# Transposing q and k of chunks 4 to 7 by DMA in a fused attention and ELU kernel, with eight shared PSUM banks and a new order of work

## The chip, the core and the metric

The kernel runs on one core of a Trainium2 chip. A core has five engines that run side by side: TensorE (PE, with its weight loads shown as PEld), VectorE (DVE), ScalarE (ACT), GpSimd (POOL) and SyncE (SP). Sixteen DMA engines move data between HBM and the on-chip memory SBUF. Matrix products land in PSUM, which has eight banks. The metric is device microseconds of one execution, as the median of several.

## The reference

The reference is a linear attention with decay, followed by a two-layer network with an ELU. All inputs are float32: q, k, v of shape (4, 8, 768, 64) for 4 batches, 8 heads, 768 positions and head size 64; a decay lam for each head; weights of 512x2048 and 2048x512.

```python
for b in range(nb):                       # blocks of 64 positions
    intra = einsum('bhic,bhjc->bhij', qb, kb) * Dmask
    intra = einsum('bhij,bhjd->bhid', intra, vb)
    inter = einsum('bhid,bhde->bhie', qb * lam_pow, kv_state)
    out[:, :, sl] = intra + inter
    kv_state = lam_block * kv_state + einsum('bhsd,bhse->bhde', kb * rev_pow, vb)
x = out.transpose(0, 2, 1, 3).reshape(3072, 512)
h = x @ w_in
g = where(h > 0, h, exp(min(h, 0)) - 1)
return g @ w_out
```

## The kernel before

The kernel cuts the 768 positions into 6 blocks of 128, so that there are 24 chunks of 128 tokens: chunk g belongs to batch g mod 4 and block g div 4. The state of a batch goes from chunk g to chunk g + 4. Chunks 0 to 3 are worked alone, and from chunk 4 on two chunks are loaded, and go through the network's first layer, as a pair (`GROUPS`, `LOADS`). Everything is float16 between float32 accumulations.

The order of all work is written out by hand in one string, `PROGRAM`, and the loop at L453 emits one word after another; no scheduler changes it. Each engine runs its own words strictly in that order and waits, by semaphore, for what a word needs. The words, with the chunk or tile in their number:

- `Lq`, `Lk`, `Lv` (L240): POOL issues a load of q, k or v that casts float32 to float16; `wi`, `wo` (L245, L251) load one of eight tiles of each weight the same way. All of these share one DMA queue, q0 on the page. `Hq0` and `Cq0` load q of chunk 0 raw from SP and cast it on DVE.
- `T`, `Tq`, `Tk` (L264): PE transposes q and k, four 128x128 blocks for each, into PSUM; `tq` (L272) moves q to SBUF on DVE, scaled by the decay `qs`, and `tk` (L276) moves k on ACT. They need the identity `idn` (L193), which needs the two `iota` of POOL.
- `Dq`, `Dk` (L280): instead, SP issues a DMA transpose from SBUF to SBUF, once the load has landed. q then is not scaled by `qs`, and the scaling is done when the chunk's result is moved (L328, on DVE; where q was scaled already, L326 on ACT moves it). Chunks 8 to 23 go this way. These transposes and the stores share the queue q1.
- `S` (L287) the scores, `s` (L294) the mask on DVE, `P` (L304, L310) the products with v and with the state, `p` (L326 or L328) the result to SBUF as `xt`.
- `kd` (L332) and `M` (L342) decay k and the state on POOL; `U` (L354, L366) the state's update on PE, `u` (L379, L381) its addition on DVE; `z` clears a state.
- `A` (L392): a part of the first layer, one PSUM bank of 512 columns; `x` (L400) exp and `r` (L403) relu on ACT, `m` (L408) the ELU on DVE into `g`.
- `B` (L422): a quarter of the second layer of a chunk, in a bank that the chunk keeps for all four; `o` (L431) moves it to SBUF, `st` (L436) stores it from SP. `R` is the last 128 columns of the last chunk.

A word after `@` names the PSUM bank. Before, A takes one of two banks of its own by turns ("H"), and the other words name one of M0, M1, A, B, C and D. The tiles `qn2`, `kn2`, `vn2` of pairs have four buffers each, `qT` and `kT` five: a word that takes a buffer waits for the last reader of the tile that had it.

Of the kernel before, what the change touches and what calls it, by code (L numbers as in the profile page):

```python
# [7 lines left out]
FP32 = mybir.dt.float32  # L8
FP16 = mybir.dt.float16
# [8 lines left out]

BUFS = {'qn1': 4, 'kn1': 4, 'vn1': 4, 'qn2': 4, 'kn2': 4, 'vn2': 4, 'qT': 5, 'kT': 5, 'pp': 6, 'kd': 8, 'stt': 8, 'xt1': 4, 'xt2': 2, 'xt4': 2, 'e': 3, 'g': 40, 'osb512': 4}

ON = {'z0.0', 'z2.0', 'z1.0', 'o23', 'z3.0'}

# [4 lines left out]


PROGRAM = (
# [53 lines left out]
)  # L85


# [1 line left out]
def kernel(  # L89
# [11 lines left out]
    nc = tc.nc  # L101
# [8 lines left out]
    FB = 4  # L110
# [48 lines left out]
        return sb.tile(shape, dtype, tag=tag, name=name, bufs=BUFS.get(tag, 1))  # L159

    def bank(tag, shape, dtype, name):
        return ps.tile(shape, dtype, tag=f"ps{tag}", name=name, bufs=2 if tag == "H" else 1)

    def ln(_):
        nc.scalar.activation(loglam[:], lam_b[:], AF.Ln)
# [216 lines left out]
                out=new, in0=stt.pop((g, hh))[r], in1=psU.pop((g, hh)), op=ALU.add  # L382
            )

    def first_product(g0, j):
        n = size_of[g0]
        assert {f"p{g0 + i}" for i in range(n)} <= done
        pH = psH[g0, j] = bank("H", [128, FB * 128], FP32, f"psH{g0}_{j}")
        for f in range(FB // n):
            i, w = divmod(j * (FB // n) + f, 2)  # L390
            for kk in range(NHP):
                nc.tensor.matmul(  # L392
                    pH[:, f * n * 128 : (f + 1) * n * 128],
                    lhsT=wi16[i][:, kk, w * 128 : (w + 1) * 128],
                    rhs=xg[g0][:, kk, :], start=(kk == 0), stop=(kk == NHP - 1),
                )
# [38 lines left out]
        t0 = b * S + c * L  # L435
        nc.sync.dma_start(out=out[t0 : t0 + 128, cols], in_=osb.pop((g, cols.start))[:])  # L436

    rest = []

    def last_columns(banks):  # L440
        cols = slice(CUT, DM)
# [11 lines left out]
    for word in words:  # L453
# [15 lines left out]
        elif kind in ("tq", "tk"):  # L469
            evacuate_t(kind[1], *a)  # L470
        elif kind in ("Dq", "Dk"):
            transpose_dma(kind[1], *a)
        elif kind == "S":
            scores(*a, banks)
        elif kind == "P":
            products(*a, banks)
        elif kind == "U":
            update_products(a, banks)
        elif kind == "B":
            second_product(*a, banks)  # L480
        elif kind == "o":
            evacuate_o(*a, psM.pop(*a)[:, cols_of(*a)], cols_of(*a), name in ON)
        elif kind == "st":
            store(*a, cols_of(*a))
        elif kind == "R":
            last_columns(banks)
        elif kind == "oR":
            evacuate_o(LAST, rest[0][:], slice(CUT, DM), False)
        elif kind == "stR":
            store(LAST, slice(CUT, DM))  # L490
        else:
            {
                "wi": load_wi, "wo": load_wo, "z": zero_state, "s": masked, "p": evacuate_p,
                "kd": decay_k, "M": decay_state, "u": update, "A": first_product, "x": exp,
                "r": relu, "m": elu,
            }[kind](*a)

# [29 lines left out]
```

## Time and profile before

| what | value |
| --- | --- |
| median of 3 runs | 215.63 us (215.39 to 217.02) |
| the profiled execution's own time | 215.01 us |
| its span, first to last instruction | 213.2 us |
| matmuls | 2048, mean granted clock 1.0 |
| first matmul, end of the last | 6.13 us, 210.13 us |
| DMA moved | 24.59 MB, 101976 packets |

The profile is of one execution. Busy time of an engine is the time in which it had an instruction in work; PE's instructions overlap, so that a busy PE says when it had work and not how fast it went. The distance from start to start of two words on PE, where nothing was waited for, says what a word costs. The view of waits says, for each instruction that its engine stood idle for, what came last before it started. The DMA share counts the packets' own times over 16 engines; packets of two queues overlap, and it can be over 1. "Landing" of a DMA is the time at which its completion is seen.

### The profile page before, as it was taken

The page shows a single profiled execution, that of the slowest core. Times are in us where ns is not written, and L with a number is a line of the kernel's source. Part 1 is how long each engine was busy: PE and PEld are TensorE (multiplying, and loading weights), DVE is VectorE, ACT ScalarE, POOL GpSimd, SP SyncE. Part 2 cuts the span into 40 slices and gives each one's busy share as a digit, 9 for nine tenths or more (in the row PEclk, how much of TensorE's full clock was granted, in tenths as well). Part 3 has the DMA queues.
Part 4 walks back from the last instruction along what each step waited for, and adds up shares of the span by engine and source line. Part 5 has one row for each costly group of instructions (what it writes and reads, how often), then busy time and mean ns, then how long its engine had stood idle before and what let it go on. Part 6 is the DMA issues. An engine that isn't in the chain of part 4 may idle for free.

```text
span 213.2 us, 5052 instructions
## 1 busy us (share of the span) xinstructions
PE 199.2 (93%) x2048; PEld 138.5 (65%) x2048; DVE 129.6 (61%) x223; ACT 127.9 (60%) x245; POOL 96.6 (45%) x115
## 2 busy tenths in 40 slices
PE   0599989999999999999989999999999999999994
PEld 0378767677677766767657677667666776666662
DVE  3877764385877866788538676366558665353321
ACT  4436766568776765585554865665674565556731
POOL 7999965599994995376902691000000000000000
PEclk9999999999999999999999999999999999999999
DMA  5999999999999999969997999146110000021042
GB/s 95 152 181 184 197 194 182 158 145 151 161 120 166 127 169 150 148 101 113 187 148 80 158 187 127 25 130 145 25 52 0 0 16 36 3 103 46 0 152 98
DMA packets 101976, 24.59 MB, mean 115 GB/s; under 512 B 92608, under 2 KB 99008, under 8 KB 101952
## 3 DMA queue, kind: packets, MB, share of 16 engines
q0 software_dynamic: 79760, 13.50, 83.5%
q1 hardware_dynamic: 22192, 10.76, 23.9%
q8 instruction: 16, 0.26, 0.5%
q14 instruction: 8, 0.07, 0.1%
HBM read 27.27 MB, written 6.29 MB: 157 GB/s over the span
## 4 chain that ended last, share of the span: by engine, by line
PE 64%; POOL 17%; DMA 15%; issue 1%; ACT 0%; SPq 0%; POOLq 0%
PE psM L422 29%; PE psH L392 28%; DMA kn<-in_k_dram 5%; DMA vn<-in_v_dram 4%; DMA qT<-qn 4%; POOL wi L245 3%; POOL kn L240 3%; POOL wo L251 3%; POOL kd L332 3%; DMA out_dram<-osb 3%; POOL qn L240 3%; PE psO L304 2%; POOL vn L240 2%; PE psO L310 2%; PE psS L287 2%
## 5 line engine op out<-in xcount | busy, mean ns | idle before, releaser
L408 DVE SCALAR_TENSOR_TENSOR g<-e,psH 128x512 f16<-128x512 f32 x96 | 65.6, 685 | 61.3 <-ACT psH L403 61.0
L392 PE MATMUL psH<-xt,wi 128*128 128x256 f16 (+1 forms) x896 | 97.6, 259 | 0.9 <-DMA wi<-in_moe_w_in_dram 0.8
L400 ACT ACTIVATE e<-psH 128x512 f32<-128x512 f32 x96 | 57.2, 596 | 67.4 <-PE psH L392 67.0
L422 PE MATMUL psM<-wo,g 128*128 128x512 f16 (+1 forms) x384 | 92.7, 377 | 0.2 <-ACT osb L431 0.2
L392 PEld LDWEIGHTS <-wi 128*128 128x128 f16 x896 | 77.5, 99 | 22.8 <-DMA wi<-in_moe_w_in_dram 1.3
L403 ACT ACTIVATE psH<-psH 128x512 f32<-128x512 f32 x96 | 56.9, 594 | 0.0
L422 PEld LDWEIGHTS <-g 128*128 128x128 f16 x384 | 36.4, 98 | 31.4 <-issue 0.4
L294 DVE TENSOR_TENSOR pp<-psS,mask 128x512 f16<-128x512 f32 x48 | 31.4, 682 | 7.6 <-PE psS L287 7.5
L332 POOL TENSOR_TENSOR kd<-kn,ks 128x512 f16<-128x512 f16 x20 | 20.8, 1049 | 13.0 <-DMA kn<-in_k_dram 12.5
L342 POOL TENSOR_TENSOR stt<-st,upp 64x256 f32<-64x256 f16 x32 | 19.6, 612 | 7.4 <-DVE st L381 5.9
L240 POOL DMA_DIRECT2D vn<-in_v_dram x14 | 15.7, 1121 | 9.0 <-PE psO L310 9.0
L431 ACT COPY osb<-psM 128x512 f32<-128x512 f32 x23 | 13.4, 588 | 5.7 <-PE psM L422 4.8
L240 POOL DMA_DIRECT2D kn<-in_k_dram x14 | 15.5, 1107 | 1.6 <-DMA wi<-in_moe_w_in_dram 1.4
L240 POOL DMA_DIRECT2D qn<-in_q_dram x13 | 14.4, 1110 | 0.1
L381 DVE TENSOR_TENSOR st<-stt,psU 64x256 f16<-64x256 f32 x32 | 13.0, 415 | 0.8 <-PE psU L366 0.3
L304 PE MATMUL psO<-pp,vn 128*64 128x128 f16 x192 | 12.5, 229 | 0.3 <-DMA vn<-in_v_dram 0.3
L304 PEld LDWEIGHTS <-vn 128*64 128x64 f16 x192 | 10.0, 114 | 2.6 <-issue 1.6
L328 DVE TENSOR_TENSOR xt<-psO,qs 128x512 f16<-128x512 f32 x16 | 10.7, 683 | 1.1 <-PE psH L392 0.6
L287 PE MATMUL psS<-qT,kT 64*128 64x128 f16 x192 | 8.4, 228 | 2.8 <-DMA qT<-qn 1.1
L310 PE MATMUL psO<-qT,st 128*64 128x128 f16 x160 | 10.3, 219 | 0.0
L287 PEld LDWEIGHTS <-kT 64*128 64x128 f16 x192 | 5.9, 98 | 5.8 <-issue 3.6
L310 PEld LDWEIGHTS <-st 128*64 128x64 f16 x160 | 9.0, 110 | 0.0
(45 smaller groups left out, 65.1 us busy)
## 6 DMA issues: line engine op xcount, KB each, us to landing
out_dram<-osb SPq DMA_DIRECT2D x23, 256.0 KB, 2.9
qn<-in_q_dram POOLq DMA_DIRECT2D x10, 256.0 KB, 8.0
kn<-in_k_dram POOLq DMA_DIRECT2D x10, 256.0 KB, 6.5
vn<-in_v_dram POOLq DMA_DIRECT2D x10, 256.0 KB, 7.0
wi<-in_moe_w_in_dram POOLq DMA_DIRECT2D x8, 256.0 KB, 6.4
wo<-in_moe_w_out_dram POOLq DMA_DIRECT2D x8, 256.0 KB, 7.4
kn<-in_k_dram POOLq DMA_DIRECT2D x4, 128.0 KB, 4.7
vn<-in_v_dram POOLq DMA_DIRECT2D x4, 128.0 KB, 5.5
```

Source lines behind the costliest of these rows:

```text
L240: nc.gpsimd.dma_start(out=t[:].rearrange("p b h d -> p (b h) d"), in_=source(w, g0, load_n[g0]))
L287: nc.tensor.matmul(psS[g, hh][:, hp, :], lhsT=tr["k", g][r, hp, :], rhs=tr["q", g][r, hp, :], start=True, stop=True,)
L294: nc.vector.tensor_tensor(out=p[:], in0=psS.pop((g, hh))[:], in1=mask[:, hh::2, :], op=ALU.mult)
L304: nc.tensor.matmul(po[r, hp, :], lhsT=of("v", g)[:, 2 * hp + hh, :], rhs=pp[g, hh][:, hp, :], start=True, stop=(cb == 0), skip_group_check ...
L310: nc.tensor.matmul(po[r, hp, :], lhsT=st[b][cb % 2][:, hp, r], rhs=tr["q", g][:, hp, :], start=False, stop=True, skip_group_check=True,)
L332: nc.gpsimd.tensor_tensor(out=kds[g][:], in0=of("k", g), in1=ks[:].unsqueeze(2).broadcast_to([128, H, 64]), op=ALU.mult,)
L342: nc.gpsimd.tensor_tensor(out=t[r], in0=st[b][cb % 2][r, :, r], in1=upp[r].unsqueeze(2).broadcast_to([64, NHP, 64]), op=ALU.mult,)
L392: nc.tensor.matmul(pH[:, f * n * 128 : (f + 1) * n * 128], lhsT=wi16[i][:, kk, w * 128 : (w + 1) * 128], rhs=xg[g0][:, kk, :], start=(kk = ...
L400: nc.scalar.activation(es[g0, j][:], psH[g0, j][:], AF.Exp)
L403: nc.scalar.activation(psH[g0, j][:], psH[g0, j][:], AF.Relu)
L408: nc.vector.scalar_tensor_tensor(out=g[:].rearrange("p f c t -> p (f c t)"), in0=es.pop((g0, j))[:], scalar=-1.0, in1=psH.pop((g0, j))[:], ...
L422: nc.tensor.matmul(psM[g][:, cols], lhsT=gts[g, f], rhs=wo16[i][:, w, cols], start=f == 0, stop=f == NFT - 1, skip_group_check=True,)
```

## The change

In the new `PROGRAM`, the words `T4` to `T7`, `tq4` to `tq7` and `tk4` to `tk7` are gone, and `Dq4` to `Dq7` and `Dk4` to `Dk7` stand in their place; thereby `p4` to `p7` are of the scaling form on DVE (L328). The loads of q, k and v of chunks 0 to 3 stand first, five of them ahead of the iotas; most of `wo` comes later than before. A names its bank like all other words, and the eight banks 0 to 7 are used by all. The order of nearly all words is a new one: sixteen A of chunks 0 to 3 now stand together ahead of their B. The functions for words `W` and `wz` are added, and no such word is in the program. Buffers, tiles and every instruction's shape stay the same.

```diff
+WARM = []
...
 PROGRAM = (
-    "lam Hq0 wi1 iota Lk0 Lk1 Lq1 Lq2 row pos0 tab Lv1 Lk2 Lv0 wi0 wo0 ln Lv2 wo1 wi2 wi3 pos1 "
-    "pos2 ks kd0 Lk3 llp qs Cq0 z2.0 kd2 kd1 Lq3 wi4 wi5 wo3 wo2 wi7 z0.0 dn wi6 kd3 Lv3 idn "
-    "Tq0@D tq0 cau Tk0@M0 tk0 S0@M1,D Tk1@B Tq1@A tk1 up msk s0.1 s0.0 tq1 S1@B,M1 Tk2@A s1.1 "
...
-    "A3:0 x3:0 o1 B0:3 r3:0 o0 T4@D T5@A tk5 Lv8 tq4 m3:0 tk4 tq5 B2:3 A3:1 S4@M0,B M4 Lk10 "
...
-    "x4:2 r4:2 m4:2 A4:4 s7.0 s6.0 s6.1 Dk8 Dq11 P7@C kd4 x4:5 r4:5 m4:5 x4:4 U4_5@A M7 P6@B "
...
+    "lam Hq0 Cq0 Lk3 Lq1 Lk0 Lq3 Lk1 iota Lq2 Lk2 tab ln pos1 dn pos2 ks wi0 Lv0 wi1 Lv3 Lv2 Lv1 "
+    "wi3 kd0 wi2 kd3 wi4 wi5 wi7 z0.1 llp wi6 z3.0 wo1 pos0 row qs idn Tk0@0 tk0 Tq0@1 cau msk "
+    "tq0 S0@2,3 s0.0 T3@4 tq3 tk3 Tq1@5 Tk1@6 Tq2@7 Tk2@0 S3@1,2 tq1 s0.1 tk1 S1@5,4 tq2 tk2 P0@6 "
+    "p0 S2@3,0 s3.1 U0@7 kd1 Lq4 Dq5 s3.0 Dq4 s2.1 s2.0 A0:0@2 P3@6 U3@1 P2@0 p3 z1.0 p2 A3:0@3 "
+    "s1.1 s1.0 wo0 P1@4 p1 Lk4 x3:0 A2:0@6 x2:0 r3:0 m3:0 Dk4 Dk5 A1:0@5 u0.1 x1:0 r1:0 A0:1@0 "
...
+    "wo4 wo6 wo7 wo3 A1:2@0 u0.0 x0:0 r0:0 m0:0 A2:2@6 r3:1 A2:3@4 z2.1 m3:1 wo2 M4 z1.1 "
+    "r3:2 x2:2 r2:2 m3:2 A2:1@1 U1@7 u1.1 x2:3 r2:3 m2:3 Lq6 A1:3@2 A0:2@3 x1:2 u1.0 kd4 x0:2 "
+    "r1:2 r0:2 m2:2 m1:2 m0:2 A3:3@5 x3:3 r3:3 z2.0 Dq6 Dq7 A0:3@4 B0:0@7 B2:0@6 m3:3 B3:0@0 "
+    "B1:0@3 B1:2 B2:2 B0:2 B3:3 Lv4 Lk6 kd5 kd2 x2:1 z0.0 r2:1 x0:3 r0:3 m0:3 x1:3 r1:3 m1:3 B0:3 "
+    "B1:3 m2:1 B2:1 B3:2 S4@5,4 S5@2,1 s4.0 s4.1 s5.1 s5.0 B2:3 B3:1 U2@5 P4@4 Lk8 o3 Lq10 Lq8 "
+    "U4_5@1 P5@2 B1:1 Dk7 o1 M5 p4 p5 A4:3@0 o2 Lq12 Lk10 x4:3 Dk6 st1 Dk8 Dk9 Lv8 kd8 A4:6@4 "
+    "x4:6 r4:3 r4:6 m4:6 m4:3 A4:2@2 A4:1@3 x4:1 Lv6 r4:1 u4.1 kd6 kd9 B0:1 Lk12 x4:2 m4:1 r4:2 "
...
+    "m4:7 A4:5@3 x4:4 x4:5 r4:5 r4:4 B4:0@7 M8 Lv10 B5:0@6 B5:1 Dq9 Dq8 B5:3 m4:4 u2.0 S7@2,1 "
+    "S6@4,0 s7.1 m4:5 B4:1 s6.1 B4:3 s7.0 B4:2 o4 s6.0 S8@5,1 s8.0 S9@3,0 U8_9@2 P7@4 s9.0 s9.1 "
+    "s8.1 P6@7 B5:2 st0 Lk14 Dq11 Dk11 Dq13 P9@5 P8@3 U6_7@0 p6 p7 S11@1,7 A6:2@4 p8 x6:2 r6:2 "
...
+    "r8:3 S10@0,1 r6:3 M11 s10.1 s10.0 m6:3 B6:0@6 B6:2 st4 Dk14 Dq12 m6:7 M12 M10 x8:0 A8:5@1 "
+    "B6:1 m8:3 Lv20 B6:3 Dk17 x8:5 r8:5 m8:5 r8:0 m8:0 Lv22 kd13 S12@0,2 S13@5,7 o6 P10@1 P11@6 "
...
     def bank(tag, shape, dtype, name):
-        return ps.tile(shape, dtype, tag=f"ps{tag}", name=name, bufs=2 if tag == "H" else 1)
+        return ps.tile(shape, dtype, tag=f"ps{tag}", name=name, bufs=1)
...
-    def first_product(g0, j):
+    def first_product(g0, j, banks):
...
-        pH = psH[g0, j] = bank("H", [128, FB * 128], FP32, f"psH{g0}_{j}")
+        pH = psH[g0, j] = bank(banks[0], [128, FB * 128], FP32, f"psH{g0}_{j}")
...
+    def make_zeros(_):
+        idle.append(const("zeros", [128, 512], FP16))
+        nc.vector.memset(idle[0][:], 0.0)
...
+    def zeros_product(k, banks):
...
+        elif kind == "A":
+            first_product(*a, banks)
+        elif kind == "W":
+            zeros_product(*a, banks)
```

More of the change, by code (lines that the diff above doesn't have):

```diff
@@ L19 @@
 BUFS = {'qn1': 4, 'kn1': 4, 'vn1': 4, 'qn2': 4, 'kn2': 4, 'vn2': 4, 'qT': 5, 'kT': 5, 'pp': 6, 'kd': 8, 'stt': 8, 'xt1': 4, 'xt2': 2, 'xt4': 2, 'e': 3, 'g': 40, 'osb512': 4}
-ON = {'z0.0', 'z2.0', 'z1.0', 'o23', 'z3.0'}
+WARM = []
+ON = {'z3.0', 'z0.0', 'z2.0', 'o23', 'z1.0'}
 PROGRAM = (
[53 rows of a table removed]
[54 rows of a table added]
 )
@@ L436, in store @@
         nc.sync.dma_start(out=out[t0 : t0 + 128, cols], in_=osb.pop((g, cols.start))[:])
-    rest = []
+    rest, idle = [], []
+    def make_zeros(_):
+        idle.append(const("zeros", [128, 512], FP16))
+        nc.vector.memset(idle[0][:], 0.0)
+    simple["wz"] = make_zeros
+    def zeros_product(k, banks):
+        if k == 0:
+            idle.append(bank(banks[0], [128, 512], FP32, "psW"))
+        nc.tensor.matmul(
+            idle[1][:, : WARM[k]], lhsT=idle[0][:, :128], rhs=idle[0][:, : WARM[k]],
+            start=True, stop=True,
+        )
     def last_columns(banks):
@@ L493 @@
                 "wi": load_wi, "wo": load_wo, "z": zero_state, "s": masked, "p": evacuate_p,
-                "kd": decay_k, "M": decay_state, "u": update, "A": first_product, "x": exp,
+                "kd": decay_k, "M": decay_state, "u": update, "x": exp,
                 "r": relu, "m": elu,
```

86 rows, old and new, of the table PROGRAM are left out of this document.

## The prediction

> **What bounds the kernel now.** The page comes first: busy shares, clock and DMA by slice, and the queues.
>
> ```profile
> PE 199.2 (93%) x2048; PEld 138.5 (65%) x2048; DVE 129.6 (61%) x223; ACT 127.9 (60%) x245; POOL 96.6 (45%) x115
> ...
> PEclk9999999999999999999999999999999999999999
> DMA  5999999999999999969997999146110000021042
> ...
> q0 software_dynamic: 79760, 13.50, 83.5%
> q1 hardware_dynamic: 22192, 10.76, 23.9%
> ```
>
> TensorE (PE) is busy 93% at full granted clock, so it sets the end; but the DMA engines show nines for the first 100 us, with q0, the POOL loads, holding most of it. Next, the stretches of 5 us (columns: stretch, length, busy PE, PEld, DVE, ACT, POOL, clock, DMA share, GB/s) tell where PE idles:
>
> ```profile
> 0.00:5.00 5.00, 0.00 (x0) 0.00 (x0) 1.29 (x7) 2.31 (x5) 3.86 (x10) 1.00 0.51 88
> 5.00:10.00 5.00, 2.64 (x24) 1.88 (x24) 4.04 (x7) 2.40 (x8) 5.00 (x7) 1.00 2.27 154
> 10.00:15.00 5.00, 3.94 (x48) 3.00 (x47) 3.52 (x6) 2.18 (x5) 4.93 (x7) 1.00 1.78 174
> 30.00:35.00 5.00, 4.22 (x62) 3.31 (x61) 1.50 (x3) 2.85 (x7) 3.42 (x3) 1.00 1.31 201
> 55.00:60.00 5.00, 4.67 (x96) 3.60 (x89) 4.36 (x7) 3.61 (x8) 4.69 (x7) 1.00 1.95 157
> 105.00:110.00 5.00, 3.91 (x41) 2.73 (x40) 2.39 (x4) 2.43 (x5) 1.91 (x2) 1.00 2.41 145
> ```
>
> Some 8.4 us are idle before 15 us, 2.5 later. The table of waits, PE's rows alone (total, times, longest), names what ended the later ones: loads and DMA transposes.
>
> ```profile
> PE psTq L264 <- DVE ident L193: 6.1, 1, 6.1
> PE psS L287 <- DMA qT<-qn: 1.1, 1, 1.1
> PE psH L392 <- DMA wi<-in_moe_w_in_dram: 0.8, 1, 0.8
> PE psO L304 <- DMA vn<-in_v_dram: 0.3, 1, 0.3
> ```
>
> The last of them is in the chain of waits, where POOL and DMA pieces carry the chain until 58 us:
>
> ```profile
> 50.37 7.86 DMA vn<-in_v_dram
> ```
>
> The load of v for chunks 6 and 7 lands at 58.23, and PE sat waiting for it. So PE bounds the whole, and up to 60 us the load queue is only just ahead of it.
>
> **PE's own work.** In the timeline, start to start without a wait, a first-product word (A) takes 0.87 us, a second-product word (B) 0.87 (0.65 in the last chunk), the eight transposes of a chunk (T) 0.45, scores 0.28 a chunk, a late chunk's products (P) 0.50, updates of a pair 0.27, and 0.10 is lost at each change from A or B to S, P or U. Summed over PE's order, before is 194.2 us and after 191.9: four T go (1.8) and some changes. Before: first matmul 6.1 + 194.2 + 9.8 of loss + 3.1 of tail (last eviction and store) = 213.2, the span. The measured time of that execution is 1.8 above its span (215.0), itself 0.6 below the median of the runs, 215.6.
>
> **The head.** POOL issues five loads (0.88 each) ahead of the two iotas, so iota_r ends at 6.05, not 2.56. DVE then runs pos1, pos2, a memset (0.27), the loglam_p copies (0.56), pos0, row, ident (0.76): the identity is ready at 8.05, not 6.08. causT and mask (0.39 + 1.23) now stand ahead of the first qT eviction (0.68), so the first scores start at 10.45, not 8.56. Then DVE holds eleven operations of 0.68 (three qT, eight masked) until 18.8; the first A waits for p0 and starts at 16.5, not 14.4. In exchange all four chunks' transposes and scores are behind it, and 16 A follow without a wait for weights: wi lands at 12.9 to 25.7 by the queue sum below, each pair about 1 us before its use. Walking the queues this way, without waits for wo and later loads, the first P of chunk 4 comes at 45.6 with 32.8 us of PE work done; before it came at 46.96 with 33.2. The loss until there is 45.6 - 8.1 - 32.8 = 4.7, against 46.96 - 6.1 - 33.2 = 7.6; less the 2.0 of a later first matmul, the head gains 0.9.
>
> **What is hidden.** ACT loses four kT copies and four P evictions (8 x 0.60 = 4.8 us); DVE swaps four qT evictions (0.69) for four scaled ones (0.68). Neither is on the path. The run of 16 A costs ACT 1.0 us each (two operations, 0.50 apart), more than PE's 0.87; its last elu is done at about 38 and read at 40: covered by 2 us. Eight banks for all cost nothing: a bank comes back 2.0 us after its A (0.17 + 0.6 + 0.5 + 0.7), and the order returns to a bank after four words, 3.5 us. kd4 and kd8 on POOL now wait for their loads, with Lv4 and Lv6 behind them; the queue still has weights or loads to move, so that costs nothing. On SP the eight new transposes hold the queue 1.2 us each, with the first stores and Dk8 behind them, at a time when SP otherwise waits for loads.
>
> If no load were late, the end would be 8.1 + 4.7 + 191.9 + 3.1 = 207.8 (before's 2.1 us of waits after that point gone too).
>
> **What is late next.** Loads share the engines with DMA transposes. The DMA view of the stretch 36 to 42 us has loads alone:
>
> ```profile
> q0 software_dynamic: 7262, 0.92, 243.9%
> ```
>
> and that of 50 to 60 us has both:
>
> ```profile
> q0 software_dynamic: 7035, 0.89, 148.4%
> q1 hardware_dynamic: 2672, 0.64, 50.7%
> ```
>
> Alone, loads move 7262 packets in 6 us, 1210 per us. In the mixed 10 us, 7035 packets are worth 5.8 us, so 2672 transpose packets cost 4.2; one transpose has 544 in the trace's packet records: 0.85 us of load time each. I take that value: it is measured under the same load. The lower end is its packets' own time (512 x 18 ns / 16 = 0.58), the upper the same sum for 62 to 70 us (1.09, after 0.93 for a store). It cannot be below nothing, since the packets occupy the same engines.
>
> Landings of back-to-back loads are 0.87 us apart for one chunk, 1.33 for a weight tile, 1.68 for a pair. Test on before: 5.0 start + 11 x 0.87 + 16 x 1.33 + 11 x 1.68 + 4 x 0.85 = 57.8, against 58.23 measured for that v load. After, the same load stands behind one more pair, 12.5 transposes (chunks 4 to 9 and the first of 11) and two stores: 5.0 + 0.45 (iotas) + 9.6 + 21.3 + 20.2 + 10.6 + 1.9 = 69.0. PE would want it, for P7, at 63.2. PE waits 5.8 us in all: about 2 already at the B words (wo2, the last weight, lands at 43.1 and is wanted at 41), the rest at S8 to P7. Then Dq12 stands on SP behind Dk15, whose k lands at 82.2; it is issued at 85.4 and lands 5.1 to 5.5 later (the median of the page's qT row is 5.1), at 90.7, while S12 is wanted at 83.6 + 5.8 = 89.4: 1.2 more. After that the words' needs lie 10 us and more behind the loads. Sum: 207.8 + 5.8 + 1.2 = 214.8 span, 216.5 us with the 1.8: **0.7% above this execution, 0.4% above the median**. A gain of 5.4 us on PE is given back to the DMA queue.
>
> [...]
>
> **The rivals.**
> - *Transposes slip between loads.* At 0.58 us each the v load lands at 65.6, P7 waits 2.4, S12 nothing: 210.2 span, 212.0 us. For it: the packets of q, k and v loads are 128 B each and a load alone moves only 158 GB/s, where weights reach 204. Against: the 50 to 60 us row, where loads fell to 58% of their rate. Chance 0.23.
> - *PE goes cold (slower).* In before, matmuls of 128 columns run 0.107 us apart until 16.07 and 0.054 after, though the granted clock is 1.00 throughout; it took 4.9 us of dense work. If the wait around S8 to P7 (3.8 us with 0.9 of work within) sends PE back to that pace for the same 4.9 us, half of them is lost: 216.5 + 2.5 = 219.0 us. It decides from an idle stretch longer than any in before after 16 us (1.1 us), so before doesn't show it. Chance 0.20. [...]
> - *Transposes cost 1.09 each.* Then the v load lands at 72, S12's q at 95.5: 8.8 + 3.1 of waits, 219.7 span, 221.5 us. For it: the 62 to 70 us row. Against: a store lies in that stretch, whose price is a guess from the same row. Chance 0.12.
>
> That the transposes don't move is excluded: the words T4 to T7 are gone and Dq4 to Dk7 are there.
>
> **How the numbers follow.** The forecast has 0.43, with a range of its own of 214 to 218.5. Faster by over 1% (below 213.5, about what a measurement of this kernel can tell from no change) is the first rival: 0.23. Slower by over 1% (above 217.8) is the second and third, and the upper edge of the forecast, 0.06: 0.38. Within 1%: 0.39 with what is left. The range, 212 to 221, reaches the first rival's end and nearly the third's.
>
> **What would show it.** After: first psTq or psTk at about 8.1; PE full from 16.5 to 36; PE's waits for DMA wo near 36 to 43 (about 2 us); waits of psS or psO for DMA qT and vn between 62 and 70 (about 4 us), the v load of chunk 6 landing near 69; a wait of psS near 90; none after 100; POOL loads in flight without a pause until 85; ACT 4.8 us less busy. I'm wrong if that v load lands before 66 or after 71, if matmuls near 70 us are 0.107 apart, or if PE waits for ACT or DVE in the runs of A.

## The result and the profile after

The changed kernel takes 221.94 us (median of 4 runs, 220.9 to 222.61), beside 215.51 us for the kernel before in the same comparison: a ratio of 1.0345, with a 95% interval of 1.0307 to 1.0384. It is 3.4% slower. The prediction had 216.5 us with a range of 212 to 221, and so the time lies just above the range.

The profiled execution took 221.87 us, with a span of 220.0. Its page, first the busy shares, then the slices and the queues:

```profile
PE 197.9 (90%) x2016; PEld 138.0 (63%) x2016; DVE 128.1 (58%) x223; ACT 120.4 (55%) x237; POOL 96.5 (44%) x115
...
PE   0299999799972799999999999899999999999994
...
PEclk9999999999997699999999999999999999999999
DMA  8999999999999999999992099760502002000133
...
q0 software_dynamic: 79760, 13.50, 83.7%
q1 hardware_dynamic: 26544, 11.81, 29.7%
```

PE has 32 matmuls fewer and ACT is busy 7.5 us less, but PE's row has a hole at the thirteenth slice (66 to 71.5 us), and in this slice and the next the granted clock, which was nines in all of before, drops to 7 and 6. The queue q0 moves the same packets as before; q1 has 4352 more, 544 for each of the eight transposes. The stretches of 5 us (columns as before: stretch, length, busy PE, PEld, DVE, ACT, POOL, clock, DMA share, GB/s) show the same with numbers:

```profile
5.00:10.00 5.00, 1.01 (x8) 0.95 (x9) 3.90 (x12) 2.55 (x8) 4.96 (x8) 1.00 2.03 129
10.00:15.00 5.00, 3.95 (x50) 3.38 (x49) 4.02 (x8) 1.57 (x3) 4.93 (x7) 1.00 1.58 150
...
30.00:35.00 5.00, 5.00 (x60) 3.66 (x58) 3.95 (x7) 4.70 (x12) 4.57 (x6) 1.00 1.64 191
...
65.00:70.00 5.00, 1.06 (x20) 0.87 (x21) 0.52 (x2) 0.49 (x1) 4.01 (x4) 0.88 1.65 174
70.00:75.00 5.00, 2.80 (x50) 2.22 (x51) 2.11 (x5) 0.00 (x0) 0.58 (x2) 0.50 2.13 156
```

From 65 to 75 us PE is busy 3.9 us of 10, and in the second half of it at a clock of 0.50. The table of waits, PE's rows (total, times, longest), names what it waited for:

```profile
PE psTk L268 <- DVE ident L197: 8.4, 1, 8.4
PE psS L291 <- DMA qT<-qn: 4.1, 1, 4.1
PE psO L308 <- DMA vn<-in_v_dram: 2.5, 2, 2.2
PE psM L426 <- DMA wo<-in_moe_w_out_dram: 1.6, 3, 0.7
PE psS L291 <- DVE qT L276: 1.4, 1, 1.4
```

The second row is S8: it waited for `Dq8`, which SP issued at 61.78 and which landed at 68.89. The third is P7, which waited for the v load of chunk 6. The chain of waits (start, length, what) shows how long that load was under way:

```profile
52.81 19.89 DMA vn<-in_v_dram
```

In before the same load took 7.86 us; here it was issued 2.4 us later than there, took 19.9 us, and landed at 72.70. The load ahead of it in the queue landed at 68.61, long after this one was issued, so that the later issue is not what made it late.

**Where the time went.** Taking each word's distance to the next one on PE, less its cost without a wait (0.87 us for an A or B, 0.50 for a late P, and so on), gives the losses. After: first matmul at 8.4 + 191.9 of work + 16.6 of loss + 3.1 of tail (last eviction and store) = 220.0; the same sum for before has 6.1, 194.2, 9.8 and 3.1. So the work is 2.3 us shorter, the start 2.2 later, and the losses 6.8 us greater. Of the 16.6, 6.9 fall before P4 (48.0 us), nothing between P4 and S8, 8.5 between 63.8 and 77.7 us, and 1.1 in all that follows.

### The profile page after: what moved, and what is told of

Read it like the earlier page. It is cut to its first block, busy times and chain, and to the rows that moved or that the text cites. A ratio compares the mean times of both kernels' runs of the same rounds, so it can differ in the third digit from the quotient of the medians.

```text
span 220.0 us, 4945 instructions
## 1 busy us (share of the span) xinstructions
PE 197.9 (90%) x2016; PEld 138.0 (63%) x2016; DVE 128.1 (58%) x223; ACT 120.4 (55%) x237; POOL 96.5 (44%) x115
## 4 chain that ended last, share of the span: by engine, by line
PE 62%; DMA 19%; POOL 13%; DVE 1%; issue 1%; ACT 1%; POOLq 0%; DVEq 0%
PE psM L426 28%; PE psH L396 27%; DMA vn<-in_v_dram 9%; DMA kn<-in_k_dram 6%; DMA wo<-in_moe_w_out_dram 4%; POOL kd L336 3%; POOL wi L249 3%; PE psO L308 3%; POOL kn L244 2%; POOL vn L244 2%; PE psO L314 2%; PE psS L291 2%; POOL qn L244 1%; DVE g L412 1%; PE psU L370 1%
## 5 line engine op out<-in xcount | busy, mean ns | idle before, releaser
L412 DVE SCALAR_TENSOR_TENSOR g<-e,psH 128x512 f16<-128x512 f32 x96 | 63.4, 682 | 50.8 <-ACT psH L407 50.6
L426 PE MATMUL psM<-wo,g 128*128 128x512 f16 (+1 forms) x384 | 89.6, 379 | 1.6 <-DMA wo<-in_moe_w_out_dram 1.6
L396 PE MATMUL psH<-xt,wi 128*128 128x256 f16 (+1 forms) x896 | 89.7, 257 | 0.0
L404 ACT ACTIVATE e<-psH 128x512 f32<-128x512 f32 x96 | 56.9, 600 | 52.6 <-PE psH L396 43.1
L396 PEld LDWEIGHTS <-wi 128*128 128x128 f16 x896 | 76.7, 98 | 13.3 <-DVE xt L332 0.3
L407 ACT ACTIVATE psH<-psH 128x512 f32<-128x512 f32 x96 | 56.0, 598 | 0.0
L298 DVE TENSOR_TENSOR pp<-psS,mask 128x512 f16<-128x512 f32 x48 | 30.7, 683 | 18.1 <-PE psS L291 15.2
L244 POOL DMA_DIRECT2D vn<-in_v_dram x14 | 15.5, 1119 | 14.7 <-PE psS L291 11.5
L332 DVE TENSOR_TENSOR xt<-psO,qs 128x512 f16<-128x512 f32 x20 | 13.4, 686 | 7.2 <-PE psO L314 7.2
L308 PE MATMUL psO<-pp,vn 128*64 128x128 f16 x192 | 13.2, 230 | 2.7 <-DMA vn<-in_v_dram 2.5
L291 PE MATMUL psS<-qT,kT 64*128 64x128 f16 x192 | 8.9, 230 | 6.3 <-DMA qT<-qn 4.1
L314 PE MATMUL psO<-qT,st 128*64 128x128 f16 x160 | 11.3, 228 | 0.0
```

What stands on the lines that cost most here:

```text
L244: nc.gpsimd.dma_start(out=t[:].rearrange("p b h d -> p (b h) d"), in_=source(w, g0, load_n[g0]))
L291: nc.tensor.matmul(psS[g, hh][:, hp, :], lhsT=tr["k", g][r, hp, :], rhs=tr["q", g][r, hp, :], start=True, stop=True,)
L298: nc.vector.tensor_tensor(out=p[:], in0=psS.pop((g, hh))[:], in1=mask[:, hh::2, :], op=ALU.mult)
L308: nc.tensor.matmul(po[r, hp, :], lhsT=of("v", g)[:, 2 * hp + hh, :], rhs=pp[g, hh][:, hp, :], start=True, stop=(cb == 0), skip_group_check ...
L314: nc.tensor.matmul(po[r, hp, :], lhsT=st[b][cb % 2][:, hp, r], rhs=tr["q", g][:, hp, :], start=False, stop=True, skip_group_check=True,)
L396: nc.tensor.matmul(pH[:, f * n * 128 : (f + 1) * n * 128], lhsT=wi16[i][:, kk, w * 128 : (w + 1) * 128], rhs=xg[g0][:, kk, :], start=(kk = ...
```

## The experiments

The theory after the result: the eight new transposes take time from the load queue, so that the v load of chunk 6 and the DMA transposes around it land late; PE idles, and its clock falls. Rivals: the new order or the shared banks cost the time themselves; or the loads are merely in the wrong order.

**1. The changed order with TensorE transposes.** `Dq4` to `Dk7` are taken out, and `T`, `tq`, `tk` of chunks 4 to 7 put back in the changed kernel's order and banks (excerpt; `p4` to `p7` stay on DVE as plain copies, since q is scaled again by `tq`).

```diff
- Dq5 ... Dq4 ... Dk4 Dk5 ... Dq6 Dq7 ... Dk7 ... Dk6
+ m0:3 T4@5 tq4 tk4 x1:3 ... B0:3 T5@4 tq5 tk5 ...
+ B4:0 T7@1 tq7 tk7 ... B5:0 T6@2 tq6 tk6
```

> The new order as it is, but chunks 4 to 7 transposed on TensorE again: T4 and T5 stand among the first B words, T7 and T6 around B5:0, their evictions on DVE (q) and ACT (k); the eight DMA transposes are gone, and the results of chunks 4 to 7 are still moved by DVE, now by a plain copy. Theory 1 (the eight transposes hold up the load queue, about 1.0 us each by where the v load of chunk 6 landed in the changed kernel, 72.7 us): that load lands 8 us earlier, near 64.7, P7 starts near 65, no slow matmul after 20 us, and the end comes near 211.5 span, 213.3 us, faster than the kernel before. Rival (the new order asks for chunks 6 to 9 earlier than any load queue can give them, or is bad in itself): the load still lands after 70 and the time stays above 218 us.

Measured: 215.48 us, a ratio of 1.0063 (1.0026 to 1.01) to a before of 214.64; span 213.7. The v load landed at 60.21 and PE never waited for a DMA after the head. In its table of waits, behind the head's row, stands this:

```profile
PE psM L427 <- DVE g L413: 2.0, 2, 1.8
```

So order, banks and head alone make the kernel about as fast as before, and measured from here 6.5 us of the changed kernel's time belong to the transposes by DMA (experiment 6 sets this higher). The expected gain was missed by 2 us: B1:3 waited 1.8 us for its ELU, since DVE and ACT had the evictions `tq4`, `tk4` ahead of it.

**2. The old order with DMA transposes.** In before's order and banks, T4 to T7 are replaced by the eight `D` words (excerpt).

```diff
- T4@D T5@A tk5 ... tq4 ... tk4 tq5 ... T6 T7 tq6 tk6 tq7 tk7
+ Lk4 Dq4 Dq5 Dk4 Dk5 ... Lq6 Dk6 Dk7 Dq6 Dq7
```

> The kernel before in its own order, with only the transposes of chunks 4 to 7 moved to DMA: Dq4, Dq5, Dk4, Dk5 behind Lk4 and Dk6, Dk7, Dq6, Dq7 behind Lq6. Theory 1: eight transposes at 0.9 to 1.0 us move the v load of chunk 6 from 58.2 to 65.5 or 66.2, S4 waits some 2 us for its transposes, and the time is 220 to 223 us although PE has 2.3 us less to do. Rival (the order is the cause): 213 to 215.5 us.

Measured: 224.92 us, 1.0474 (1.0446 to 1.0501), above the 220 to 223 expected. The v load of chunk 6 landed at 66.57, near the expected time, but PE's wait was an earlier one. Its PE clock and first row of waits:

```profile
PEclk9999999965999999999999999999999999999999
```

```profile
PE psS L287 <- DMA kT<-kn: 7.9, 2, 6.6
```

S4 waited 6.6 us for the transposed k of chunk 4 (about 2 expected), and behind it the clock fell. In the old order that k landed at 40.04 and its transpose, the third on SP, at 49.52, with S4 due at 42.7; the changed order loads chunk 4 some 7 us earlier, and the same transpose landed at 44.22 for S4 at 45.02. In round numbers, with TensorE transposes 214.6 (before) and 215.5 (experiment 1), with DMA transposes 224.9 and 221.9: the transposes cost 10.3 us in the old order and 6.5 in the new (8.4 measured from experiment 6). The new order hides 2 to 4 us of them and is not what makes the kernel slow.

**3. PE kept warm through the wait.** The words `W` and `wz`, which the change defines and does not use, are put in, and the function of `W` is rewritten so that one word issues several products: 19 and 11 products of zeros, 512 columns each, into banks that are free (excerpt).

```diff
-WARM = []
+WARM = [19, 11]
-    "... S8@5,1 ... U8_9@2 P7@4 ..."
+    "... W0@2 S8@5,1 ... U8_9@2 W1@4 P7@4 ..."
```

> The changed kernel with 30 products of zeros of 512 columns put into PE's two waits (19 ahead of S8, 11 ahead of P7), in banks that are free there, and one memset of the zeros on DVE; nothing else moves. Theory 2 (the wait lets PE fall to half pace, which costs 1.6 us between S8 and P8): matmuls from 69 to 77 us run at full pace, the v load still lands near 72.7, and the time is 220.3 us. Rival (the half pace is only seen while PE waits anyway): 221.9 us, unchanged. The products must not end after the loads land; if they do by some tenths, that much is to be taken off.

Measured: 220.48 us, 1.0273 (1.024 to 1.0306). The v load still landed at 72.90, and the stretches read:

```profile
65.00:70.00 5.00, 5.00 (x50) 2.45 (x50) 0.77 (x2) 0.58 (x1) 3.89 (x4) 1.00 1.67 172
70.00:75.00 5.00, 4.74 (x63) 2.39 (x57) 2.38 (x5) 0.00 (x0) 0.78 (x2) 1.00 2.11 156
```

The clock stays at 1.00 and the kernel is 1.5 us faster than the changed one, though P7 still starts when the v load lands (72.94 here, 72.74 there). This shows that about 1.5 us of the changed kernel's time were the cold clock, and that it came from PE standing idle. In the changed kernel the matmuls of P7 and P6 are 0.107 us apart and those of P9, at 76 us, 0.056.

**4. Twice the transposes.** Each of the eight is issued a second time by SP into a tile that nobody reads; all else stays.

```diff
         nc.sync.dma_start_transpose(out=t[:], in_=of(w, g).rearrange("p h d -> p (h d)"))
+        if 4 <= g <= 7:
+            nc.sync.dma_start_transpose(out=const(f"twice_{w}{g}", ...)[:], in_=of(w, g)...)
```

> The changed kernel with each of the eight new DMA transposes issued twice, the second into a tile that nobody reads. Theory 1: the v load of chunk 6 moves from 72.7 by eight times the price of a transpose; 80.7 at 1.0 us each, 77.3 at the 0.58 of packets that slip between loads, 81.4 at 1.09. The time rises by about as much: 229 to 231 us at 1.0. Rival (transposes cost the loads nothing, the order does it): 222 us and 72.7.

Measured: 228.76 us (two executions), 1.066 (1.0594 to 1.0726); the v load landed at 79.97, 7.3 us later than in the changed kernel, 0.91 us for each duplicate. PE's waits, below the head's row:

```profile
PE psS L296 <- DMA kT<-kn: 5.0, 2, 3.1
PE psU L375 <- DMA vn<-in_v_dram: 3.1, 1, 3.1
PE psS L296 <- DMA qT<-qn: 2.1, 1, 2.1
PE psO L313 <- DMA vn<-in_v_dram: 1.6, 1, 1.6
```

None, eight and sixteen extra transposes: 215.5, 221.9, 228.8 us, 0.81 and then 0.85 us for each one. The second step is the clean one: PE's work and every other word stay, nobody reads the duplicates, and yet the end moves by 6.8 us, with all of PE's new waits for DMA and a lower mean clock behind them (0.963 against 0.982). That time on the DMA engines is the cause is thereby shown. In the first step the transposes also take 1.8 us of work off PE, and experiment 1 has a badly placed eviction, so that the two steps are alike in part by luck. The duplicates hold SP's queue as well, so that this run does not part late issue from late landing in the waits for qT and kT; the v load is not issued by SP.

**5. Loads in the order of need.** `Lq8` moves ahead of `Lq10`, and `Lv8`, `Lv6` ahead of `Lk10`, `Lq12`.

```diff
-    "... Lk8 o3 Lq10 Lq8 ... o2 Lq12 Lk10 ... Lv8 kd8 ... Lv6 ..."
+    "... Lk8 o3 Lq8 Lq10 ... o2 Lv8 Lv6 ... kd8 Lk10 ... kd6 Lq12 ..."
```

> The changed kernel with five load words moved on POOL and nothing else: Lq8 ahead of Lq10, and Lv8, Lv6, Lk10, Lq12 in this order where Lq12, Lk10, Lv8, Lv6 stood. The transposes stay on DMA. Theory 1 (P7 waits for a place in the load queue): the v load of chunk 6 stands behind two pair loads less (2 x 1.68) and two transposes less, and lands near 67.5 instead of 72.7; S8 starts near 66, P7 near 68, and S11 then waits 2 to 3 us for the k of chunk 10, now later. The time is 216 to 219 us. Rival (the wait is a matter of the transposes' own latency, wherever the loads stand): P7 still after 72, 221.9 us.

Measured: 221.93 us, 1.0335 (1.0293 to 1.0377): no gain. The v load did land 3.9 us earlier, at 68.85, and S8 waited 0.8 us only; but:

```profile
PE psS L292 <- DMA kT<-kn: 3.6, 2, 3.4
PE psO L309 <- DMA vn<-in_v_dram: 2.1, 1, 2.1
```

S11 then waited for its k, whose load had been put back (it landed at 70.57, its transpose at 76.83). The wait moved and did not shrink (0.8, 2.1 and 3.6 us in this execution, the fastest of the four, against 4.1, 2.5 and 0.2 in the changed kernel): the queue as a whole was late, and not one load in a bad place. The expected 216 to 219 was wrong for that reason.

**6. TensorE transposes, better placed.** Experiment 1 with the evictions `tq4`, `tk4` behind the ELU that had waited for them, and T7, T6 one B later.

```diff
-    "... m0:3 T4@5 tq4 tk4 x1:3 r1:3 m1:3 ... B5:0 T6@2 ..."
+    "... m0:3 T4@5 x1:3 r1:3 m1:3 tq4 tk4 ... B5:0@6 T7@1 tq7 tk7 B5:1 T6@2 ..."
```

> The new order with chunks 4 to 7 on TensorE, as in the first run of this kind, in which B1:3 waited 2.0 us for its ELU because the evictions of chunk 4 stood ahead of it on DVE and ACT, and T7 waited 0.5 us for a bank. Here these evictions stand behind that ELU, and T7 and T6 one B word later. Theory: both waits go, 2.5 us less: 213.0 us, about 1% faster than the kernel before. Rival (other words wait in their place): 215 us or more.

Measured: 213.55 us, 0.9944 (0.9917 to 0.997) of a before of 214.88. It is the fastest version besides the next, 0.6% faster than before and 3.9% faster than the changed kernel (0.9944 against 1.0345). Measured from here the eight transposes cost 8.4 us: the 6.5 of experiment 1 is too small by the 2 us that its own badly placed evictions cost, which the changed kernel does not have. What is left of its waits on PE is small:

```profile
PE psS L292 <- ACT kT L281: 0.5, 1, 0.5
PE psM L427 <- DVE g L413: 0.5, 1, 0.5
PE psM L427 <- DMA wo<-in_moe_w_out_dram: 0.2, 1, 0.2
```

The v load landed at 61.80, 4.4 us ahead of P7 (66.24).

**7. The same with an earlier first score.** `Tq0` and `tq0` go ahead of the mask.

```diff
-    "... idn Tk0@0 tk0 Tq0@1 cau msk tq0 S0@2,3 ..."
+    "... idn Tq0@1 Tk0@0 tk0 cau tq0 msk S0@2,3 ..."
```

> As the one before it, and in the head q of chunk 0 is transposed ahead of k, and its eviction stands ahead of the mask on DVE. S0 starts 0.5 us earlier, DVE's row of masked scores 0.3 to 0.4 us earlier: 212.6 us. Rival (DVE's row, not S0, sets the first A, and the mask is as late as before): no difference.

Measured: 213.3 us, 0.9952 (0.9919 to 0.9985), the same as experiment 6 within the intervals, as the rival had it. S0 did start 0.66 us earlier, at 10.08, but the first A started at 15.73 in both: here the matmuls of the head were 0.107 us apart until 15.7, in experiment 6 until 14.0 only. At 21 us A0:1 then waited 0.5 us for its tile of `wi`, which it had not done there. So the earlier score was given back, once to the slow start of PE and once to the loads.

**8 and 9. Half of the transposes.** Experiment 6, with only chunks 6 and 7 by DMA (8), or only chunks 4 and 5 (9), at the changed kernel's places. Since the v load stood 4.4 us ahead of its use, four transposes might fit.

```diff
 experiment 8
-    "... B5:0@6 T7@1 tq7 tk7 B5:1 T6@2 tq6 tk6 ..."
+    "... z2.0 Dq6 Dq7 ... B1:1 Dk7 ... x4:3 Dk6 ..."
 experiment 9
-    "... T4@5 ... tq4 tk4 ... T5@4 tq5 tk5 ..."
+    "... Lq4 Dq5 s3.0 Dq4 ... m3:0 Dk4 Dk5 ..."
```

> The kernel of e6 with q and k of chunks 6 and 7 transposed by DMA, at the changed kernel's places (Dq6, Dq7, Dk7, Dk6), chunks 4 and 5 still by TensorE. PE has 0.9 us less work. In e6 the v load of chunk 6 landed at 61.8, 4.4 us ahead of P7 at 66.2, and Dq8 at 62.6, 2.8 us ahead of S8 at 65.4. Theory (a transpose costs the load queue 0.8 to 1.0 us and nothing else until the slack is gone): four put the v load at 65.2 to 65.8, wanted at 65.3, and Dq8 at about 66, wanted at 64.5, so that PE waits some 1 to 2 us at S8 or S11: 213.6 - 0.9 + 1.5 = 214.2 us. Rival (each transpose costs the end 0.8 us, whatever stands there): 216.8 us. Rival (these four slip between loads): 212.7 us.

> The kernel of e6 with q and k of chunks 4 and 5 transposed by DMA (Dq5, Dq4, Dk4, Dk5 at the changed kernel's places), chunks 6 and 7 by TensorE. These four share the engines mostly with weight loads, beside which a transpose cost about 0.65 us in the changed kernel. Theory: the v load of chunk 6 lands at 61.8 + 2.6 = 64.4, Dq8 at 65.2, against needs of 65.3 and 64.5: the wait is under 1 us, and P4 is 0.5 to 1.5 later as the wo loads are later; 213.6 - 0.9 + 1.2 = 213.9 us, a little below the run with chunks 6 and 7 by DMA. Rival (0.8 us each at the end): 216.8 us. Rival (hidden): 212.7 us.

Measured: 217.71 us, 1.0113 (1.0076 to 1.015), and 217.73 us, 1.0121 (1.0071 to 1.017). The theory's 214 fell, and the rival's 216.8 was nearer: four transposes cost 4.2 us (3.6 to 3.8 by the ratios to before), about half of what eight cost against the same experiment 6 (8.4, or 8.6 by the ratios). The v load landed at 69.37 and 70.56, that is 7.6 and 8.8 us later than in experiment 6 for four transposes. The price of 0.65 us for the early ones did not hold either: with two of the four done and two in work, the last weight landed 2.5 us later than in experiment 6 (43.35 against 40.83). The landings show the rest. In experiment 6 three transposes had landed by then and a fourth was in work (3.5), and one store; in 8 and 9 it was ten transposes and two stores. SP issues the transposes of chunks 8 to 11 and the stores when their own inputs are ready, whether the loads are late or not, so each microsecond that the v load is delayed lets more of them get ahead of it. Four were added, and 7.5 transfers more came first: 1.2 us each in experiment 9. The same sum for the changed kernel against experiment 6 gives 14 transposes and 2 stores, 11.5 more for 10.9 us: 0.95 each. In experiment 8 the 7.6 us hold another cost too. In POOL's waits from 30 to 62 us stands

```profile
POOL qn L245 <- DMA qT<-qn: 8.1, 1, 8.1
```

The load of q for chunk 12 waited 8.1 us for a buffer of q, until `Dq7` had landed (51.76), and the queue ran nearly dry behind it: 173 load packets from 52 to 54 us, where loads alone make 2460.

The two also differ in the clock. Experiment 8, then 9, in the stretch with the wait and the one behind it:

```profile
65.00:70.00 5.00, 1.37 (x44) 1.15 (x40) 1.35 (x3) 0.47 (x1) 4.71 (x7) 0.77 2.02 125
70.00:75.00 5.00, 5.00 (x78) 3.40 (x75) 2.62 (x5) 0.00 (x0) 4.92 (x6) 0.55 2.42 157
```

```profile
65.00:70.00 5.00, 2.49 (x40) 1.27 (x37) 3.05 (x5) 0.58 (x1) 3.90 (x4) 1.00 2.03 127
70.00:72.50 2.50, 1.89 (x36) 1.23 (x36) 1.28 (x3) 0.00 (x0) 0.99 (x1) 1.00 2.46 157
```

P7 waited 3.6 us in the first and 3.1 us in the second; the first went cold and lost 2.3 us more in the words that follow (5.9 us from P7 to the next A, against 3.6). The second did not: the trace of experiment 9 holds no clock record, but its matmuls of P7 are 0.056 us apart. It lost 1.0 us of this again in two waits for a transposed k at 136 us.

## Why the prediction was wrong, step by step

Two of the signs that the prediction named for its being wrong came: the v load landed after 71, and the matmuls near 70 us were 0.107 us apart. The third, PE waiting for ACT or DVE in the runs of A, did not. A small slip: its own sum, 214.8 + 1.8, is 216.6 and not 216.5.

**PE's work and the head: right.** First matmul 8.37 (8.1 predicted), S0 10.73 (10.45), first A 16.07 (16.5), work 191.9, as predicted. From 16.5 to 36 us PE had no wait. The waits for `wo` at B words came to 2.1 us (0.55, 0.86, 0.66) where about 2 was forecast, and the loss until P4 was 6.9 us against 4.7 + 2.0. All that stands ahead of 63.8 us is therefore within 0.5 us, the shift of the first matmul included.

**What was hidden: right.** PE waited for no ACT or DVE operation in the runs of A; ACT is 7.5 us less busy by the page, 4.8 of it the eight operations that were forecast; the other 2.7 were not followed, since ACT is on no path here. The shared banks cost nothing that a row shows.

**The load queue: the step that failed.** The mechanism was the right one; the term of the transposes in the queue sum was too small. The prediction put "12.5 transposes (chunks 4 to 9 and the first of 11) and two stores" ahead of the v load, 0.85 us for a transpose, which made 69.0 us. It landed at 72.70, behind 14 transposes and 2 stores. Up to the last weight the sum came out, though by two errors: it landed at 43.16 (43.1 predicted), with the early loads 1.2 us later than forecast and only 2.5 transposes done instead of four. Behind it ten pair loads of 1.68 us (16.8) took 29.5 us. The other 12.7 went to 2 stores (1.9 at the prediction's price) and 11.5 transposes, where the forecast had 8.5: so 0.94 us each. Three transposes more make 2.8 of the 3.7 us behind the last weight, and the higher price 0.8. Half of these three had been forecast ahead of the last weight, where their absence hid that the early loads were 1.2 us late; counted over the whole sum, the 3.7 us are therefore about 1.2 of late early loads, 1.3 of 1.5 transposes more, and 1.2 of a higher price for all 14. The 1.5 more are those of chunk 11: the forecast held SP's issues fixed and counted what they put ahead of a load that lands at 69.0; it did not ask what gets ahead while it is late. The DMA view of the changed kernel for 48 to 64 us (packets, MB, share of 16 engines) bears the price out:

```profile
q0 software_dynamic: 11291, 1.43, 144.1%
q1 hardware_dynamic: 3408, 1.05, 50.1%
```

At 1210 load packets per us, 11291 are worth 9.3 us of the 16; 6.7 us went to 3408 packets, 1.07 us for 544 with a store among them. The packets' records show how they share: in the 2 us from 56, 839 load packets and 840 of q1, equal numbers, where loads alone make 2460.

**S8 and P7.** PE waited 4.1 us at S8 and 2.2 more at P7. With the words between them, which ran at the slow pace, P7 came 7.1 us after its turn; the prediction had 3.8 for the two. S8 was late because its own transpose was: `Dq8` took 7.1 us to land and the others near it 7.4 to 8.5, where the prediction took 5.1 to 5.5 for a transpose.

**The cold clock: the mechanism was right, its place in the list was wrong.** It stood as a rival beside the forecast and beside the rival of dear transposes, though here it came with the longer waits that dear transposes made (0.50 from the end of the one at S8 on, 1.00 in experiment 3 with PE kept at work). It cost 1.5 us (experiment 3) against 2.5 estimated. The start of before, which it was worked out from, was misread a little: the pace changed at 16.3 us and not at 16.07, from 0.107 to 0.056 us, and the trace has no clock record ahead of 16.31, so that the 1.00 of the rows before it measures nothing. The two rivals came true together; the dear transposes alone gave 221.5, with 3.1 of waits at S12 that didn't come.

**S12: wrong in sign.** `Dq12` landed at 94.45, later than the predicted 90.7, but PE itself was 5 us late by then, and nothing waited. S19 lost 0.7 us at 138 us that was not foreseen; experiment 1 loses 0.6 at the same word.

The sum: 214.8 of predicted span + 0.3 (first matmul) + 0.2 (until P4) + 3.3 (P7 late by 7.1 and not 3.8) + 1.4 (the slow pace from P7 on) - 0.1 (the rest: 1.1 against 1.2) = 219.9, against 220.0.

**The other rival**, transposes that slip between loads (212.0), is excluded by experiments 4, 8 and 9, where none of them was free.

What stays open: what part of a transpose's price is its packets' own time and what comes on top was not measured by itself. The 1.5 us of the cold clock are those of this wait at this place; in other runs the clock stood at 0.50 for a shorter or a longer time (last section).

## What to carry to other kernels

Price work that is moved from a compute engine to the DMA queues at the most loaded stretch of the load queue, and ask what else is issued on time while the loads run late: in experiments 8 and 9 four added transposes put 7.5 transfers more ahead of the late load, so that the slack in its landing was used up about twice as fast as by the added ones alone (4.4 us of slack did not hold four transposes). Where a forecast has PE idle for some microseconds on end, put the cold clock into the sum rather than beside it: here it cost 1.5 us, with waits of 4.1 and 2.2 us. A change that joins a good part (here the order, 0.6% faster than before once two evictions were moved) with a bad one is worth taking apart before it is judged.

## What the runs showed of the hardware

- Two DMA queues that both had work moved nearly equal numbers of packets in the two stretches that were counted, though their packets differ in size: 323 of the loads and 319 of the transposes from 36 to 38 us of the changed kernel, with weight packets of 1024 B, and 839 and 840 from 56 to 58 us, with 128 B packets; the transposes' are of 256 B. Alone, weight loads moved some 470 packets in 2 us (939 in the 4 us from 30 of before) and the 128 B loads 2460. So the former kept about two thirds of their rate, and the latter, with the smaller packets, one third.
- The granted clock fell behind some of PE's waits and not behind others, and the longest wait alone did not tell which. It stood at 0.50 for 6.83 us in the changed kernel, from 68.79, where the wait of 4.1 us at S8 ended; for about 6.8 us in experiment 8 (0.77 and 0.55 in the rows above), where P7 waited 3.6 us; and for 3.41 us in experiment 5, where the waits at S8 and P7 were of 0.8 and 2.1 us. In experiment 2, where S4 waited 6.6 us, it reads 6 and 5 tenths in two slices of 5.6 us. It stayed at 1.00 in experiment 5 at the wait of 3.4 us at S11; and in experiment 9 the matmuls behind the wait of 3.1 us at P7 are 0.056 us apart, the full pace. The lengths between its changes in the traces of before (197.97 us) and of the changed kernel (54.61, 6.83 and 143.36) are whole multiples of 3.41 us. These are stretches of that length in experiment 5, ahead of the fall (PE idle for 2.24 us), in it, and with most of the wait at S11 that comes later (PE idle for 1.83):

```profile
64.81:68.22 3.41, 1.17 (x33) 0.87 (x32) 1.66 (x3) 0.59 (x1) 2.33 (x3) 1.00 1.74 164
68.22:71.63 3.41, 2.74 (x35) 2.02 (x36) 1.75 (x3) 0.00 (x0) 0.92 (x1) 0.50 2.33 154
75.05:78.46 3.41, 1.58 (x20) 1.36 (x21) 0.75 (x2) 0.17 (x1) 1.25 (x3) 1.00 1.84 155
```

  The executions of one kernel differed too: of the six of experiment 9, three have a mean granted clock of 0.991 or 0.992 and three of 0.998 or more. The idle times rest on PE's busy time, whose ends are modelled, so that they are rough.
- A DMA's time to land grew from 5.8 us for a pair load on a nearly empty queue (experiment 8, issued at 52.32) to 19.9 us for the v load of the changed kernel, with the same bytes.
